# Stages of the experts in pairs, with the low parts of some first weights set apart, and two early waits

## The chip, the cores and the metric

The kernel runs on one core of a Trainium2 chip. The metric is the device time of one execution in microseconds (us). The engines are named as the profile names them: PE is TensorE (matrix products), PEld its weight loads, DVE VectorE, ACT ScalarE, POOL GpSimd, SP the engine that issues the DMAs.

## The reference

Three layers run one after the other on 1152 tokens with 512 features. The lines below are cut from the reference.

```python
# 1 attention on two batches of 8 heads: a pooled one (mean over 4) and a local one (|i-j| < 4)
out_d = sm_attn(q_d, k_d, v_d); out_up = np.repeat(out_d, factor, axis=2)
...
return (out_up + out_local).astype(np.float32)
# 2 a layer with sigmoid gating, 512 -> 2048 -> 512
h = x @ w_in
g = h * (1.0 / (1.0 + np.exp(-h)))
return (g @ w_out).astype(np.float32)
# 3 four experts, each 512 -> 1024 -> 512, weighted per token
for e in range(E):
    h = np.maximum(x @ w1[e], 0.0)
    out += p[:, e:e + 1] * (h @ w2[e])
```

## The kernel before

Every float32 operand of a product is held as two numbers of the fast type, a high part and a low part (`xh`, `xl`; `gh`, `gl`; `wh`, `wl`). One product of the mathematics is three instructions of PE: high weight by high data, high weight by low data, low weight by high data. Each instruction loads 128 columns of stationary weights and streams 256, 320 or 384 columns of moving data.

Layer 2 runs in two halves of the inner features (`for hf in range(2)`). A half goes over chunks of tokens. In a chunk, `g1_step` makes eight tiles of inner features (12 instructions each) and `g2_step` four tiles of the output (24 each). The first half has chunks of 256, 320, 256 and 320 tokens, the second of 256, 256, 256 and 384. The last tile of the first half goes into `acc` through ACT (L590), that of the second half through DVE (L593).

Layer 3 goes over experts e, chunks of tokens ci (three of 256 tokens, the last of 384) and stages k of 256 inner features. A stage has first products (`first_products`, 24 instructions on `mm` tiles, streaming `xh` and `xl`, with w1 stationary), a relu into `r` on ACT, seven linear combinations of token blocks and their high and low parts `h` on ACT, DVE and POOL, and second products (`second_products`: 21 instructions, 33 in the last chunk, with `h` stationary, streaming w2, into banks `p`). Seven block products stand for eight, so `outputs` adds the banks up on DVE with the weights of the tokens at the end of a chunk. The bank B[2] is read there last, by two adds into `u`. Only for ci = 3 do the first products stream 384 columns; these are called wide stages below. All second products stream 256.

The order on PE is: first products of stage n + 1, then second products of stage n. A scheduler moves instructions by priorities (`prio`, `tick_of`), so at the start of a chunk the two kinds are mixed in small pieces. The next expert's weights are split into high and low parts by `split_u` (w1) and `split_kk` (w2) while the wide stages run.

In the built program the stationary and moving operands have fixed places. Steps are told here by the address of the next weights less that of the moving data, modulo 128 bytes. Inside first products, inside second products and all through layer 2 the step is 64. It is 0 at each of the 105 switches from first to second products and at each of the 104 back.

Of the kernel before, what the change touches and what calls it, by code (L numbers as in the profile page):

```python
# [61 lines left out]
def attention_moe_kernel(ctx, tc, kqa, kqb, qtl, va, vb, w64, w1d, w2d, dpr, out):  # L62
# [33 lines left out]
    def prio(t):  # L96
        tc.cur_priority = 1000000 + int(1000 * t)
# [99 lines left out]
    def split_raw(u, j, t):  # L197
# [21 lines left out]
        else:  # L219
            c = slice(j * 1024, (j + 1) * 1024)  # L220
            behind(ACT, ACT.activation(out=h[:, c], in_=t, func=ACTF.Copy))
            behind(DVE, DVE.tensor_tensor(out=l[:, c], in0=t, in1=h[:, c].bitcast(F32), op=ALU.subtract))


    actx = ExitStack()
# [347 lines left out]
    def g1_step(u0, ft, o, n):  # L573
        c = slice(o, o + n)
        ps = mm_tile()
        for k in range(HP):
            mm3(ps[:, 0:n], g1_pairs(u0, ft, k, c), k == 0, k == HP - 1)
        g1_evac(ps, ft, n)

    def g2_step(u0, hf, db, o, n):  # L580
        c = slice(o, o + n)
        ps = mm_tile()
        for f in range(8):
            wh, wl = unit[u0 + f // 4]
# [14 lines left out]


    ks_p, pp_p, r_p, u_p, o_p2, h_p = [], [], [], [], [], []
    wk, w1k = {}, {}

    def tick_of(e, ci, k):
        return 96 + EXPERT * e + STAGE * (4 * ci + k) + (2 * k if ci == 3 else 0)

# [36 lines left out]
    def home_u(k):  # L643
        h, l = slot(8 + k // 2)
        c = slice(1024 * (k % 2), 1024 * (k % 2) + 1024)
        return h[:, c], l[:, c]

    def split_u(e, k):
        t, i = staged.pop((e, "u", k))
        h, l = w1k[k] = home_u(k)  # L650
        for c in (slice(0, 512), slice(512, 1024)):
            with at_prio(tick_of(e, 0, k) - LEAD_USPLIT):
                ACT.activation(out=h[:, c], in_=t[:, c], func=ACTF.Copy)
                eng = POOL if k in U_LO_POOL else DVE
                eng.tensor_tensor(out=l[:, c], in0=t[:, c], in1=h[:, c].bitcast(F32), op=ALU.subtract)
        held[i] -= 1
        stage_ahead()

# [32 lines left out]
    def first_products(st):  # L691
        e, ci, k = st.at
        t = 2 * ci
        st.r = r_p[0].tile([128, 8, 128], F32, tag="r", name="r")
        st.h = [h_p[0].tile([128, 7, 128], F32R, tag=f"h{i}", name=f"h{i}") for i in range(2)]
        if ci == 3:
            st.o = [o_p2[0].tile([128, 2, 128], F32R, tag=f"o{i}", name=f"o{i}") for i in range(2)]
            tiles = [mm_tile() for _ in range(2)]
            for half in range(2):
                prio(tick_of(*st.at) + 1.5 * half)  # L700
                m1_products(tiles[half][:, 0:384], k, half, slice(128 * t, 128 * t + 384))
        else:
            ps = mm_tile()
            for half in range(2):
                prio(tick_of(*st.at) + half)
                m1_products(ps[:, 256 * half:256 * half + 256], k, half, slice(128 * t, 128 * t + 256))
        p = tick_of(*st.at) + (3 if ci == 3 else 2) - LEAD_PAIR
        r = st.r
        with at_prio(p):
# [8 lines left out]
                                             op0=ALU.max, op1=ALU.subtract)  # L718
            else:
                ACT.activation(out=r[:, 0:4].rearrange("p s t -> p (s t)"), in_=ps[:, 0:512], func=ACTF.Relu)  # L720
        for n, (part, d) in enumerate(((slice(1, 4), 0.0), (slice(4, 8), 1.0))):
            with at_prio(p + d):
                if n == 1:
# [13 lines left out]
    def prod(ps, hs, terms, k, opens):  # L737
        wh, wl = wk[k]
        pairs = []
        for a, b in terms:  # L740
            h, l = hs[0][:, a], hs[1][:, a]
            pairs += [(h, wh[:, b]), (h, wl[:, b]), (l, wh[:, b])]
        n = len(pairs)
        ins = [PE.matmul(out=ps, lhsT=x, rhs=y, start=(opens and k == 0 and i == 0), stop=(k == 3 and i == n - 1),  # L744
                         skip_group_check=True) for i, (x, y) in enumerate(pairs)]
        return ins[0]

    def second_products(st, ch):
        e, ci, k = st.at
# [9 lines left out]
        first = {}  # L759
        for t, i, hs, terms in groups:  # L760
            m = prod(half(t, i), hs, terms, k, i == 0)
            if k == 0:
                if i == 0:
                    first[id(t)] = m
                else:
                    after(m, first[id(t)])

    def scaled_add(o, ps, p, first=False):
        if first:
# [155 lines left out]
    class Chunk:  # L925
        pass

    def finish(st, ch, p):
        e, ci, k = st.at
        prio(p)  # L930
        second_products(st, ch)
        if ci == 3 and e < NE - 1:
            split_kk(e + 1, k)
            if k < 2:
                sum_ahead(e + 1, k + 2)
        if k == 3:
            outputs(e, ci, ch, p)

    before = None
    for e in range(NE):  # L940
        for ci in range(4):
            ch = Chunk()
            for k in range(4):
                st = Stage()
                st.at = (e, ci, k)
                first_products(st)
                if ci == 3 and e < NE - 1:
                    split_u(e + 1, k)
                if ci == 2 and k % 2 == 0 and e < NE - 1:
                    sum_ahead(e + 1, k // 2)  # L950
                if before:
                    finish(*before, tick_of(e, ci, k) + (3 if ci == 3 else 2))
                before = (st, ch)
    finish(*before, tick_of(NE, 0, 0) + 2)


# [54 lines left out]
```

## Time and profile before

| What | Value |
|---|---|
| median of 3 runs | 679.53 us (675.22 to 679.6) |
| the profiled execution | 679.06 us, its span 677.1 us |
| granted TensorE clock, mean | 0.989 |
| PE busy | 652.2 us, 96% of the span |
| layer 2, second half | about 188 to 290 us of the span |
| the experts | about 290 to 670 us |

The span runs from the first to the last instruction; the rest of the execution's time lies outside it. PE has an instruction in flight nearly all the time, so its busy share does not tell how fast it goes. What tells it is the distance from one start of a PE instruction to the next, which is read from the start times of the timeline.

### The profile page before, as it was taken

The numbers are of one execution on the slowest core, as the hardware profiler recorded it, in microseconds if no ns is written. First come the engines' busy times: TensorE is split into PE (matmuls) and PEld (weight loads), VectorE is DVE, ScalarE is ACT, GpSimd is POOL, SyncE is SP. The second block draws the span as 40 slices with busy tenths as digits, with TensorE's granted clock in tenths as the row PEclk, the third lists the DMA queues.
The fourth block names the chain that finished last, engine by engine and source line by source line (L and its number), as shares of the span: only waits on it lengthen the run. The fifth ranks groups of instructions, "written<-read, shape, count | busy, mean of one in ns | idle before, by whom it ended". The sixth has DMA issues, their size and how long they took to land.

```text
span 677.1 us, 13739 instructions
## 1 busy us (share of the span) xinstructions
PE 652.2 (96%) x5516; PEld 636.4 (94%) x5516; DVE 418.6 (62%) x850; ACT 330.6 (49%) x753; POOL 245.1 (36%) x346
## 2 busy tenths in 40 slices
PE   4879999999999999999999999999999999999995
PEld 4668988998999999999999999999999999999995
DVE  4668575474645544765548865668854668755434
ACT  2898765478844434352335633346533356433321
POOL 5536641133600000652356323545422554333210
PEclk9898999999999999999999999999999999999998
DMA  8964612116501200140003310013300020000001
GB/s 265 364 224 146 210 39 62 25 47 203 170 18 32 94 1 1 63 156 1 1 1 100 119 33 1 1 32 125 95 1 1 1 64 1 1 33 32 1 32 47
DMA packets 16927, 48.16 MB, mean 71 GB/s; under 512 B 2976, under 2 KB 4256, under 8 KB 16864
## 3 DMA queue, kind: packets, MB, share of 16 engines
q1 hardware_dynamic: 16864, 47.29, 21.8%
q8 instruction: 43, 0.70, 0.4%
q14 instruction: 20, 0.16, 0.1%
HBM read 44.93 MB, written 2.36 MB: 70 GB/s over the span
## 4 chain that ended last, share of the span: by engine, by line
PE 82%; DMA 5%; ACT 4%; DVE 4%; POOL 3%; issue 1%; SPq 0%; ACTq 0%; POOLq 0%
PE mm L540 53%; PE p L744 26%; DMA stg<-in_w_dram 3%; DVE dec L210 1%; DMA vg_f<-in_va_dram 1%; ACT dec L208 1%; PE s L369 1%; DMA vg<-in_va_dram 1%; POOL wbuf L218 1%; POOL kq L306 1%; PE t L432 1%; DVE acc L772 1%; PE o L464 1%; ACT wbuf L217 0%; ACT stg L209 0%
## 5 line engine op out<-in xcount | busy, mean ns | idle before, releaser
L540 PE MATMUL mm<-xh,wbuf 128*128 128x256 f32 (+2 forms) x1280 | 269.4, 297 | 5.5 <-DVE gf L560 3.6
L540 PEld LDWEIGHTS mm<-xh,wbuf 128*128 128x128 f32 x1280 | 210.9, 190 | 7.7 <-DVE gf L560 5.2
L540 PE MATMUL mm<-xl,wbuf 128*128 128x256 f32 (+2 forms) x640 | 189.6, 297 | 0.0
L726 POOL TENSOR_TENSOR r<-r 128x128 f32<-128x128 f32 x160 | 93.4, 596 | 183.7 <-ACT r L720 144.1
L729 DVE TENSOR_TENSOR h<-r,h 128x384 fp32r<-128x384 f32 (+1 forms) x128 | 91.7, 720 | 64.6 <-ACT h L728 64.3
L540 PEld LDWEIGHTS mm<-xl,wbuf 128*128 128x128 f32 x640 | 121.6, 190 | 0.2
L728 ACT ACTIVATE h<-r 128x384 fp32r<-128x384 f32 (+1 forms) x128 | 73.2, 577 | 85.0 <-POOL r L726 53.9
L540 PE MATMUL mm<-gh,wbuf 128*128 128x256 f32 (+2 forms) x512 | 103.5, 296 | 1.0 <-DVE gf L560 0.9
L744 PE MATMUL p<-wext,h 128*128 128x256 f32 x672 | 91.5, 279 | 0.0
L744 PE MATMUL p<-wbuf,h 128*128 128x256 f32 x672 | 84.6, 278 | 0.0
L744 PEld LDWEIGHTS p<-wext,h 128*128 128x128 f32 x672 | 84.4, 188 | 0.0
L540 PEld LDWEIGHTS mm<-gh,wbuf 128*128 128x128 f32 x512 | 82.3, 188 | 1.5 <-DVE gf L560 1.1
L744 PEld LDWEIGHTS p<-wbuf,h 128*128 128x128 f32 x672 | 81.2, 188 | 0.0
L540 PE MATMUL mm<-gl,wbuf 128*128 128x256 f32 (+2 forms) x256 | 74.2, 295 | 0.0
L720 ACT ACTIVATE r<-mm 128x512 f32<-128x512 f32 x48 | 28.7, 597 | 76.1 <-PE mm L540 75.7
L726 DVE TENSOR_TENSOR r<-r 128x128 f32<-128x128 f32 x96 | 33.6, 351 | 37.6 <-ACT r L720 33.0
L566 DVE TENSOR_TENSOR gl<-gf,gh 128x256 fp32r<-128x256 f32 (+2 forms) x64 | 37.6, 589 | 18.9 <-ACT gh L565 18.1
L540 PEld LDWEIGHTS mm<-gl,wbuf 128*128 128x128 f32 x256 | 47.8, 188 | 0.0
L218 POOL TENSOR_TENSOR wbuf<-dec,wbuf 128x512 fp32r<-128x512 f32 x24 | 32.0, 1351 | 24.9 <-ACT wbuf L217 18.8
L772 DVE SCALAR_TENSOR_TENSOR acc<-p,pr,acc 128x256 f32<-128x256 f32 (+1 forms) x63 | 36.1, 605 | 5.9 <-PE p L744 5.9
L671 POOL TENSOR_TENSOR wext<-kst,wext 128x512 fp32r<-128x512 f32 x8 | 10.7, 1342 | 79.9 <-ACT wext L669 44.3
L560 DVE SCALAR_TENSOR_TENSOR gf<-th,mm 128x256 f32<-128x256 f32 (+2 forms) x64 | 28.4, 450 | 17.7 <-ACT th L559 16.2
(138 smaller groups left out, 940.8 us busy)
## 6 DMA issues: line engine op xcount, KB each, us to landing
stg<-in_w_dram SPq DMA_DIRECT2D x25, 512.0 KB
kst<-in_w2d_dram SPq DMA_DIRECT2D x16, 512.0 KB
kst<-in_w1d_dram SPq DMA_DIRECT2D x12, 512.0 KB
acc<-in_w_dram SPq DMA_DIRECT2D x7, 512.0 KB
kq<-in_kqb_dram SPq DMA_DIRECT2D x8, 323.0 KB
kq<-in_kqa_dram SPq DMA_DIRECT2D x6, 419.0 KB
stg<-in_w1d_dram SPq DMA_DIRECT2D x4, 512.0 KB
vw<-in_vb_dram SPq DMA_DIRECT2D x8, 180.0 KB
```

The source lines that it names most:

```text
L208: first = ACT.activation(out=d, in_=v[:, :, 1].bitcast(F32), func=ACTF.Prelu, scale=2.0 ** -112, alpha=2.0 ** 32)
L218: POOL.tensor_tensor(out=l[:, c], in0=d, in1=h[:, c].bitcast(F32), op=ALU.subtract)
L540: ins = [PE.matmul(out=ps, lhsT=l, rhs=r, start=(first and i == 0), stop=(last and i == n - 1)) for i, (l, r) in enumerate(pairs)]
L560: DVE.scalar_tensor_tensor(out=gf[:, 0:n], in0=th[:, 0:n], scalar=1.0, in1=ps[:, 0:n], op0=ALU.add, op1=ALU.mult)
L566: latest[DVE] = DVE.tensor_tensor(out=gl[ft][:, 0:n], in0=gf[:, 0:n], in1=gh[ft][:, 0:n].bitcast(F32), op=ALU.subtract)
L671: b = eng.tensor_tensor(out=l[:, r], in0=x, in1=h[:, r].bitcast(F32), op=ALU.subtract)
L720: ACT.activation(out=r[:, 0:4].rearrange("p s t -> p (s t)"), in_=ps[:, 0:512], func=ACTF.Relu)
L726: latest[eng] = eng.tensor_tensor(out=r[:, o], in0=r[:, a], in1=r[:, b], op=op)
L728: ACT.activation(out=h, in_=r[:, part], func=ACTF.Copy)
L729: latest[DVE] = DVE.tensor_tensor(out=l, in0=r[:, part], in1=h.bitcast(F32), op=ALU.subtract)
L744: ins = [PE.matmul(out=ps, lhsT=x, rhs=y, start=(opens and k == 0 and i == 0), stop=(k == 3 and i == n - 1), skip_group_check=True) for i, ...
L772: DVE.scalar_tensor_tensor(out=o, in0=ps, scalar=p, in1=o, op0=ALU.mult, op1=ALU.add)
```

## The change

Four things change. Stages go in pairs: first products of two stages, then second products of the pair before, in a fixed order (`emit` chains every product of layer 3 behind the one before). That leaves 31 switches from first to second products and 30 back. For the first stage of each pair, the low part of its first 128 columns of w1 is written into a place of its own (`first_lo`), and that product goes first, so that the step at all 30 switches back is 64. The relu, the combinations and the `o` buffers (three now) follow the pairs. And the last tile of each half of layer 2 is moved out of PSUM in two parts, of 16 columns and the rest; the first product of the second half, and the first of the experts, waits for the 16 columns.

```diff
-            mm3(ps[:, 0:n], g1_pairs(u0, ft, k, c), k == 0, k == HP - 1)
+            i, _ = mm3(ps[:, 0:n], g1_pairs(u0, ft, k, c), k == 0, k == HP - 1)
+            if k == 0 and part_done:
+                wait_part(i)
         g1_evac(ps, ft, n)
...
+    part_done = []
+
+    def wait_part(i):
+        tc.add_manual_dep(i.ins, part_done.pop().ins.name, mybir.DependencyInfo(mybir.DependencyClass.Sync, mybir.DependencyReason.DATA),
+                          reason="part done")
...
+        last = db == 3 and o + n == NT
+        cols = (slice(0, 16), slice(16, n)) if last else (slice(0, n),)
         if hf == 0:
-            ACT.activation(out=ya, in_=ps[:, 0:n], func=ACTF.Copy, scale=0.5)
+            done = [ACT.activation(out=ya[:, a], in_=ps[:, a], func=ACTF.Copy, scale=0.5) for a in cols]
         else:
             yf = tmp_p[0].tile([128, tmp_p[1]], F32, tag="gf", name="gf")
-            DVE.scalar_tensor_tensor(out=yf[:, 0:n], in0=ps[:, 0:n], scalar=0.5, in1=ya, op0=ALU.mult, op1=ALU.add)
+            done = [DVE.scalar_tensor_tensor(out=yf[:, a], in0=ps[:, a], scalar=0.5, in1=ya[:, a], op0=ALU.mult, op1=ALU.add)
+                    for a in cols]
+        if last:
+            part_done[:] = done[:1]
...
+    def apart(k):
+        return k % 2 == 0
+
+    PAIRS = [((e, ci, k), (e, ci, k + 1)) for e in range(NE) for ci in range(4) for k in (0, 2)]
+
+    def product_ticks():
+        at, t = {}, 96
+        for n in range(len(PAIRS) + 1):
+            for what, pair in (("m", n), ("p", n - 1)):
+                for x in PAIRS[pair] if 0 <= pair < len(PAIRS) else ():
+                    at[what, x] = t
+                    t += 3 if x[1] == 3 else 2
+        return at
+
+    AT = product_ticks()
...
+    def lower(eng, k, l, h, t, c):
+        parts = [(l[:, c], c)]
+        if apart(k) and c.start == 0:
+            parts = [(w1a[k], slice(0, 128)), (l[:, 128:c.stop], slice(128, c.stop))]
+        return [eng.tensor_tensor(out=o, in0=t[:, s], in1=h[:, s].bitcast(F32), op=ALU.subtract) for o, s in parts]
...
-    def m1_products(ps, k, half, c):
+    def m1_products(ps, k, half, c, begin=False):
         wh, wl = w1k[k]
+        pairs = []
         for q in range(HP):
             s = slice(half * 512 + q * 128, half * 512 + q * 128 + 128)
-            mm3(ps, [(wh[:, s], xh[:, q, c]), (wh[:, s], xl[:, q, c]), (wl[:, s], xh[:, q, c])], q == 0, q == HP - 1)
+            if apart(k) and half == q == 0 and not begin:
+                pairs += [(w1a[k], xh[:, q, c]), (wh[:, s], xh[:, q, c]), (wh[:, s], xl[:, q, c])]
+            else:
+                pairs += [(wh[:, s], xh[:, q, c]), (wh[:, s], xl[:, q, c]), (wl[:, s], xh[:, q, c])]
+        n = len(pairs)
+        return [lambda i=i, a=a, b=b: PE.matmul(out=ps, lhsT=a, rhs=b, start=(i == 0), stop=(i == n - 1))
+                for i, (a, b) in enumerate(pairs)]
...
+        first_lo = late.tile([128, 384], F32R, name="first_lo")
+        for i in range(2):
+            w1a[2 * i] = first_lo[:, 80 + 128 * i:208 + 128 * i]
...
-    o_p2.append(moe2_pool("o2", 2))
+    o_p2.append(moe2_pool("o2", 3))
...
+    newest = []
+
+    def emit(todo, t):
+        with at_prio(t):
+            for f in todo:
+                i = f()
+                if newest:
+                    follow(i, newest[0], "order of products")
+                else:
+                    wait_part(i)
+                newest[:] = [i]
...
+    def second_stage(at):
+        e, ci, k = at
+        st = stages[at]
+        t = AT["p", at]
+        emit(second_products(st, st.ch), t)
+        prio(t)
...
+    for n in range(len(PAIRS) + 1):
+        new = []
+        if n < len(PAIRS):
+            new.append(first_stage(PAIRS[n][0]))
+            first_relu(new[0])
+            new.append(first_stage(PAIRS[n][1]))
+        for i in range(2):
+            if n:
+                second_stage(PAIRS[n - 1][i])
+            if new:
+                if i == 0:
+                    first_relu(new[1])
+                first_results(new[i])
```

On PE, at a switch from second to first products in the first expert, the rows before are these (`p` are the banks, `mm` the tile of the first products).

```order
L744 MATMUL p_4126<-wbuf,h_4208 128x256 x2
L744 MATMUL p_4126<-wbuf,h_4209 128x256
L540 MATMUL mm<-xh,wbuf 128x256
L540 MATMUL mm<-xl,wbuf 128x256
L540 MATMUL mm<-xh,wbuf 128x256 x2
```

The switch falls after second products of one stage, on weights in `wbuf`. After, at the first such switch, PE's rows are these.

```order
L797 MATMUL p_3937<-wext,h_3873 128x256 x2
L797 MATMUL p_3937<-wext,h_3874 128x256
L727 MATMUL mm<-xh,first_lo 128x256
L727 MATMUL mm<-xh,wbuf 128x256
L727 MATMUL mm<-xl,wbuf 128x256
```

The first product after the switch now takes its weights from `first_lo`, and the two with the high part follow; before it, second products of two stages stand in a row.

On DVE, at the end of the first expert's last chunk, from the first add into `u` that reads bank p_4656 (B[2]) to the second, the rows before are these (`acc<-` are the scaled adds, `wbuf<-` weight splits for the next expert, `h` a low part).

```order
L801 TENSOR_TENSOR u<-u,p_4656 128x256
L729 TENSOR_TENSOR h_4902<-r,h_4901 128x512
L671 TENSOR_TENSOR wbuf<-ks,wbuf 128x256
L772 SCALAR_TENSOR_TENSOR acc<-p_4657,pr,acc 128x256
L772 SCALAR_TENSOR_TENSOR acc<-p_4655,pr,acc 128x256
L772 SCALAR_TENSOR_TENSOR acc<-p_4657,pr,acc 128x512
L671 TENSOR_TENSOR wbuf<-ks,wbuf 128x512
L671 TENSOR_TENSOR wbuf<-kst,wbuf 128x512
L772 SCALAR_TENSOR_TENSOR acc<-u,pr,acc 128x256
L729 TENSOR_TENSOR h_4994<-r,h_4993 128x384
L805 TENSOR_TENSOR u<-u,p_4656 128x256
```

Nine operations stand between the two, no combination `r<-r` among them. After, the last part of the same stretch on DVE, with p_4736 as B[2], is this.

```order
L782 TENSOR_TENSOR h_5027<-r,h_5026 128x384
L833 SCALAR_TENSOR_TENSOR acc<-p_4737,pr,acc 128x256
L833 SCALAR_TENSOR_TENSOR acc<-p_4735,pr,acc 128x256
L833 SCALAR_TENSOR_TENSOR acc<-p_4737,pr,acc 128x512
L782 TENSOR_TENSOR h_5027<-r,h_5026 128x512
L709 TENSOR_TENSOR wbuf<-kst,wbuf 128x512
L779 TENSOR_TENSOR r<-r 128x128
L833 SCALAR_TENSOR_TENSOR acc<-u,pr,acc 128x256
L779 TENSOR_TENSOR r<-r 128x128 x2
L866 TENSOR_TENSOR u<-u,p_4736 128x256
```

Three combinations `r<-r` now stand ahead of the second add into `u`, where there were none.

On ACT, at the end of the first half of layer 2, the rows before are these.

```order
L590 ACTIVATE acc<-mm 128x320
L217 ACTIVATE wbuf<-dec 128x512
L590 ACTIVATE acc<-mm 128x320 x3
L559 ACTIVATE th<-mm 128x256
L565 ACTIVATE gh_2625<-gf 128x256
```

The four tiles of the last chunk leave in four operations. After, ACT's rows at that place are these.

```order
L602 ACTIVATE acc<-mm 128x320
L217 ACTIVATE wbuf<-dec 128x512
L602 ACTIVATE acc<-mm 128x320 x2
L602 ACTIVATE acc<-mm 128x16
L602 ACTIVATE acc<-mm 128x304
L561 ACTIVATE th<-mm 128x256
```

The last of the four tiles is moved in two parts.

## Rows read from the trace of the kernel before

**Rows 1.** The page: busy time by engine, and the chain that ended last.
```profile
PE 652.2 (96%) x5516; PEld 636.4 (94%) x5516; DVE 418.6 (62%) x850; ACT 330.6 (49%) x753; POOL 245.1 (36%) x346
...
PE 82%; DMA 5%; ACT 4%; DVE 4%; POOL 3%; issue 1%; SPq 0%; ACTq 0%; POOLq 0%
```

**Rows 2.** PE's timeline, first expert: start us, us, then line, names, shape, count.
```profile
321.45 2.64 PE L744 MATMUL p<-wext,h 128*128 128x256 f32 x21
...
323.92 0.28 PE L540 MATMUL mm<-xh,wbuf 128*128 128x256 f32 x1
...
326.65 2.55 PE L744 MATMUL p<-wbuf,h 128*128 128x256 f32 x21
...
329.04 0.28 PE L540 MATMUL mm<-xh,wbuf 128*128 128x256 f32 x1
...
331.87 2.64 PE L744 MATMUL p<-wbuf,h 128*128 128x256 f32 x21
```

**Rows 3.** PE's timeline where the second half starts and its last chunk starts.
```profile
188.04 0.31 PE L540 MATMUL mm<-gh,wbuf 128*128 128x320 f32 x1
...
188.18 0.28 PE L540 MATMUL mm<-xh,wext 128*128 128x256 f32 x1
...
256.03 0.34 PE L540 MATMUL mm<-xh,wext 128*128 128x384 f32 x1
```

**Rows 4.** PE's timeline after a wide stage, in the first and last expert.
```profile
354.25 2.63 PE L744 MATMUL p<-wbuf,h 128*128 128x256 f32 x21
...
356.71 0.34 PE L540 MATMUL mm<-xh,wbuf 128*128 128x384 f32 x1
...
662.25 1.22 PE L744 MATMUL p<-wbuf,o 128*128 128x256 f32 x9
...
666.14 1.22 PE L744 MATMUL p<-wbuf,o 128*128 128x256 f32 x9
```

**Rows 5.** Busy time in a stretch: PE, PEld, DVE, ACT, POOL, clock, DMA, GB/s.
```profile
300.00:350.00 50.00, 50.00 (x432) 50.00 (x432) 29.27 (x55) 18.42 (x34) 19.32 (x32) 1.00 0.01 2
```

**Rows 6.** PE's timeline after a wait, and after a break of other matmuls.
```profile
65.99 0.39 PE L540 MATMUL mm<-gh,wbuf 128*128 128x256 f32 x1 [0.86 <-DVE gf L560]
...
132.18 0.40 PE L540 MATMUL mm<-gh,wbuf 128*128 128x320 f32 x1
...
133.34 0.39 PE L540 MATMUL mm<-xh,wbuf 128*128 128x256 f32 x2
...
133.68 0.39 PE L540 MATMUL mm<-xh,wbuf 128*128 128x256 f32 x2
```

**Rows 7.** The timeline of all engines, where a tile leaves PSUM and PE waits.
```profile
188.38 0.44 ACT L590 ACTIVATE acc<-mm 128x320 f32<-128x320 f32 x1 [3.08 <-PE mm L540]
...
289.77 0.56 DVE L593 SCALAR_TENSOR_TENSOR gf<-mm,acc 128x384 f32<-128x384 f32 x1 [1.87 <-PE mm L540]
...
162.82 0.47 DVE L560 SCALAR_TENSOR_TENSOR gf<-th,mm 128x320 f32<-128x320 f32 x1
...
163.35 0.19 PEld L540 LDWEIGHTS mm<-xh,wbuf 128*128 128x128 f32 x1 [0.28 <-DVE gf L560]
```

**Rows 8.** Groups by line and form: busy us, mean ns; idle before.
```profile
L712 ACT ACTIVATE r<-mm 128x256 f32<-128x256 f32 x32 | 11.9, 372 | 15.8 <-PE mm L540 14.3 <-DVE acc L772 1.5
...
L716 ACT ACTIVATE o<-mm 128x128 fp32r<-128x128 f32 x32 | 8.7, 271 | 0.0
...
L717 DVE SCALAR_TENSOR_TENSOR o<-mm,o 128x128 fp32r<-128x128 f32 x32 | 9.1, 285 | 21.7 <-ACT o L716 21.7
...
L726 DVE TENSOR_TENSOR r<-r 128x128 f32<-128x128 f32 x96 | 33.6, 351 | 37.6 <-ACT r L720 33.0 <-ACT r L712 3.3
```

**Rows 9.** The timeline of DVE and PE, end of the first expert.
```profile
386.65 1.41 DVE L770 TENSOR_SCALAR acc<-p,pr 128x512 f32<-128x512 f32 x2 [0.33 <-PE p L744]
...
387.47 0.28 PE L540 MATMUL mm<-xh,wbuf 128*128 128x256 f32 x1
...
393.64 0.41 DVE L805 TENSOR_TENSOR u<-u,p 128x256 f32<-128x256 f32 x1
```

More of the change, by code (lines that the diff above doesn't have):

```diff
@@ L221, in split_raw @@
             behind(ACT, ACT.activation(out=h[:, c], in_=t, func=ACTF.Copy))
-            behind(DVE, DVE.tensor_tensor(out=l[:, c], in0=t, in1=h[:, c].bitcast(F32), op=ALU.subtract))
+            k = 2 * (u - 8) + j
+            for o, a in ((l[:, c], slice(0, 1024)),) + (((w1a[k], slice(0, 128)),) if apart(k) else ()):
+                behind(DVE, DVE.tensor_tensor(out=o, in0=t[:, a], in1=h[:, c][:, a].bitcast(F32), op=ALU.subtract))
     actx = ExitStack()
@@ L601, in attention_moe_kernel @@
     ks_p, pp_p, r_p, u_p, o_p2, h_p = [], [], [], [], [], []
-    wk, w1k = {}, {}
+    wk, w1k, w1a = {}, {}, {}
+    def apart(k):
[10 more added lines that the diff above has]
+    AT = product_ticks()
     def tick_of(e, ci, k):
-        return 96 + EXPERT * e + STAGE * (4 * ci + k) + (2 * k if ci == 3 else 0)
+        return 96 + EXPERT * NE if e == NE else AT["m", (e, ci, k)]
     todo = deque([(0, "k", k) for k in range(4)])
@@ L654, in split_u @@
                 eng = POOL if k in U_LO_POOL else DVE
-                eng.tensor_tensor(out=l[:, c], in0=t[:, c], in1=h[:, c].bitcast(F32), op=ALU.subtract)
+                lower(eng, k, l, h, t, c)
         held[i] -= 1
@@ L693, in first_products, with first_relu @@
         t = 2 * ci
+        if ci == 3:
+            st.tiles = [mm_tile() for _ in range(2)]
+            return [i for half in range(2)
+                    for i in m1_products(st.tiles[half][:, 0:384], k, half, slice(128 * t, 128 * t + 384))]
+        st.tiles = [mm_tile()]
+        return [i for half in range(2)
+                for i in m1_products(st.tiles[0][:, 256 * half:256 * half + 256], k, half, slice(128 * t, 128 * t + 256), (e, ci) == (0, 0))]
+    def first_relu(st):
+        e, ci, k = st.at
+        tiles = st.tiles
+        ps = tiles[0]
         st.r = r_p[0].tile([128, 8, 128], F32, tag="r", name="r")
-        st.h = [h_p[0].tile([128, 7, 128], F32R, tag=f"h{i}", name=f"h{i}") for i in range(2)]
         if ci == 3:
             st.o = [o_p2[0].tile([128, 2, 128], F32R, tag=f"o{i}", name=f"o{i}") for i in range(2)]
[L698 to L706, printed above, removed]
         p = tick_of(*st.at) + (3 if ci == 3 else 2) - LEAD_PAIR
@@ L720, in first_products, with first_results @@
                 ACT.activation(out=r[:, 0:4].rearrange("p s t -> p (s t)"), in_=ps[:, 0:512], func=ACTF.Relu)
+    def first_results(st):
+        e, ci, k = st.at
+        r = st.r
+        st.h = [h_p[0].tile([128, 7, 128], F32R, tag=f"h{i}", name=f"h{i}") for i in range(2)]
+        p = tick_of(*st.at) + (3 if ci == 3 else 2) - LEAD_PAIR
         for n, (part, d) in enumerate(((slice(1, 4), 0.0), (slice(4, 8), 1.0))):
@@ L743, in prod @@
         n = len(pairs)
-        ins = [PE.matmul(out=ps, lhsT=x, rhs=y, start=(opens and k == 0 and i == 0), stop=(k == 3 and i == n - 1),
-                         skip_group_check=True) for i, (x, y) in enumerate(pairs)]
-        return ins[0]
+        return [lambda i=i, x=x, y=y: PE.matmul(out=ps, lhsT=x, rhs=y, start=(opens and k == 0 and i == 0),
+                                                stop=(k == 3 and i == n - 1), skip_group_check=True)
+                for i, (x, y) in enumerate(pairs)]
     def second_products(st, ch):
@@ L758, in second_products, with opening @@
             groups.insert(5, (B[3], 1, st.o, ((0, 2),)))
-        first = {}
+        first, todo = {}, []
+        def opening(f, t, i):
+            m = f()
+            if i == 0:
+                first[id(t)] = m
+            else:
+                after(m, first[id(t)])
+            return m
         for t, i, hs, terms in groups:
-            m = prod(half(t, i), hs, terms, k, i == 0)
+            fs = prod(half(t, i), hs, terms, k, i == 0)
             if k == 0:
[L763 to L766, printed above, removed]
+                fs[0] = lambda f=fs[0], t=t, i=i: opening(f, t, i)
+            todo += fs
+        return todo
     def scaled_add(o, ps, p, first=False):
@@ L926, in attention_moe_kernel, with first_stage @@
         pass
[L928 to L931, printed above, removed]
+    newest = []
[5 more added lines that the diff above has]
+                    follow(i, newest[0], "order of products")
+                else:
+                    wait_part(i)
+                newest[:] = [i]
+    stages = {}
+    def first_stage(at):
+        e, ci, k = at
+        st = stages[at] = Stage()
+        st.at = at
+        st.ch = stages[e, ci, 0].ch if k else Chunk()
+        emit(first_products(st), tick_of(*at))
+        if ci == 3 and e < NE - 1:
+            split_u(e + 1, k)
+        if ci == 2 and k % 2 == 0 and e < NE - 1:
+            sum_ahead(e + 1, k // 2)
+        return st
+    def second_stage(at):
+        e, ci, k = at
+        st = stages[at]
+        t = AT["p", at]
+        emit(second_products(st, st.ch), t)
+        prio(t)
         if ci == 3 and e < NE - 1:
@@ L936, in finish @@
         if k == 3:
[L937 to L954, printed above, removed]
+            outputs(e, ci, st.ch, t)
+    for n in range(len(PAIRS) + 1):
[8 more added lines that the diff above has]
+            if new:
+                if i == 0:
+                    first_relu(new[1])
+                first_results(new[i])
 def kernel(**inputs):
```

1 line of the change is left out of this document (added).

## The prediction

> **What bounds the kernel now.** The page comes first: PE is busy 96% of the span, and 82% of the chain that ended last is PE [rows 1]. So the time is PE's, and the question is how far apart its products start. In the timeline of PE in the first expert, 21 second products from 321.45 us to 323.92 take 117.6 ns each, the 24 first products after them 113.8, the next 21 second products 113.8 and the 24 first products from 329.04 to 331.87 117.9 [rows 2]. Shapes and engine are the same, and the clock stays at 1.00, the upper level of 2.4 GHz [rows 5]. So there are two paces. A settled fast row of products has three products in 0.34 us, 113.3 ns each [rows 6]; the slow pace is read best from the second half of layer 2, where 576 products of 256 columns go from 188.18 to 256.03, 117.8 ns each, all slow [rows 3].
>
> What sets the pace? It lasts through steps of 64 and through the switches from first to second products: the stretch at 326.65 stays fast, as the one before it [rows 2]. It turns at switches back, slow to fast at 323.92 and fast to slow at 329.04 [rows 2]; of 46 such switches with a clear pace on both sides, all 15 out of the fast pace end slow, 20 of 31 out of the slow one end fast. After a wide stage it is slow in all 16 cases: 21 products at 117.1 ns after the first one, 33 at 117.9 after the last [rows 4]. From 320 columns straight into 256 it is slow too [rows 3], but after the same 320 columns and a break of other matmuls it is fast at 133.34 [rows 6]. In the experts the two paces mix: 432 products overlap 50 us, (50 + 0.28) / 432 = 116.4 ns [rows 5].
>
> **The change, part by part,** in the span of the profiled execution (677.1 us, with 1.96 us outside it).
>
> *The wait at the second half.* PE now stops before 188.18. The last product starts at 188.04 and takes 0.31 us [rows 3], ACT starts at 188.38 on the tile [rows 7]; 16 columns take about 0.18 us by the line through 128 columns (271 ns) and 256 (372 ns) [rows 8]. A released PE loads weights 0.06 us after the releaser's end (162.82 + 0.47 to 163.35, [rows 7]), and its product starts some 0.11 us later. That gives 188.73, 0.55 us late; the first starts after a stop are about 0.12 us slower in sum than settled ones. Price 0.67 us. ACT was idle for 3.08 us before [rows 7], so nothing stands ahead of it; on PE the whole second half is queued behind the wait. Bounds: 0.6 us, and 0.8 if 16 columns cost as much as 128. In return the half starts after a stop, so fast if the break at 132 us is the pattern: 576 x (117.8 - 113.3) = 2.6 us less. Its 384-column chunk I leave as it is.
>
> *The wait at the experts.* The same on DVE, which starts at 289.77 after 1.87 us of idling and takes 0.56 us for 384 columns [rows 7], 285 ns for 128 [rows 8], so about 0.17 for 16. Price 0.66 us. The two waits make +1.3 us.
>
> *The switches.* All 30 switches back now have the step of 64 that never turned the pace, and the 31 others never did. So a pace stays until a wide stage or a stop. With 256 columns an expert has 3 x 4 x 24 = 288 first and 12 x 21 + 4 x 33 = 384 second products, 672 in all, 2688 in four. The first expert starts fast and keeps it for 288 first products and ten stages of 21 second ones, 498 products; the first wide stage makes it slow.
>
> *A stop at the ends of experts.* Seen in the order on DVE: the sixth group of the next expert's first second products opens bank B[2], which DVE must have read twice. In the trace that queue, 13 operations, runs from 386.65 to 393.64 + 0.41, 7.4 us; first products went on at 387.47 [rows 9]. After, the same 13 and three combinations of 351 ns [rows 8] stand there, some 0.3 us each as neighbours overlap: 8.3 us, and two operations that stood behind the first scaled add now precede the second, so that it starts at about the end of PE's products, not 0.8 us before. PE arrives after 48 first and 15 second products, 63 x 117.8 ns = 7.4 us. So it waits 8.3 + 0.2 (restart as above) - 7.4 = 1.1 us, between 0 (the old lead of 0.8 us and quicker splits) and 1.6 (PE fast, 0.3 us earlier). Three such ends: +3.3 us, 0 to 4.8. At the other chunk ends the queue lacks the three splits and a scaled add, four of sixteen, so about 6.2 us against 7.4, and no stop.
>
> Each such stop also restarts PE fast. A later expert then is slow from its predecessor's wide stages to the stop (42 + 66 + 48 + 66 + 48 + 15 = 285) and fast for the other 387. With the last expert's 42 + 132 at the end: 498 + 3 x 387 = 1659 fast and 1029 slow. 1659 x 113.3 + 1029 x 117.8 = 309.2 us, against 2688 x 116.4 = 312.9: -3.7 us.
>
> *Nothing on the path:* the low parts in two pieces (some 8 more operations of 0.2 to 0.6 us on DVE and POOL, which are busy 62% and 36% [rows 1]); the pairs, which give the results of a stage more time before PE needs them. Without that cover each piece would cost its length.
>
> Sum: -2.6 + 1.3 + 3.3 - 3.7 = -1.7; 679.06 - 1.7 = **677.4 us**. The profiled execution is 0.5 us under the median of 679.53. With the bounds of the stops, 674 to 680.
>
> **A rule against the change.** The rows show two paces for the same shapes [rows 2]. The Trainium skill, page SBUF — State Buffer, section "A bandwidth-pool intuition that's wrong (but worth ruling out)", gives weight loads a second read port of their own. By that rule the place of weights cannot disturb the moving data, and setting some apart buys no pace. No row here shows ports; by it the sum would be that of the fourth rival.
>
> **The rivals.** *Fast nearly throughout.* Wide stages left it slow, but each was entered slow; entered fast, or with `first_lo` after it, the pace may hold. Then 2688 x 3.1 ns = 8.3 us less: -2.6 + 1.3 - 8.3 = -9.6 without stops (669.5 us), -5.4 with three of 1.4 (673.7). Against it: 16 of 16 [rows 4].
>
> *Slow to the end.* The stops are hidden, or a restart amid second products is not fast: from the first wide stage 2190 products are slow, +3.1 - 1.5 = +1.6: 679.4 without stops, 682.7 with them.
>
> *Slower: the new step holds the slow pace.* Fast or slow may hang on more than the step modulo 128: inside second products it is 192 or 448 modulo 512, inside first ones 64, and no row shows the one follow the other directly. If `first_lo` ends the fast pace at the first switch back, 96 first and 42 second products are fast and some 2550 slow, +3.6 - 0.4, and with a second half that stays slow too: +1.3 + 3.2 + 3.3 = 686.9 us. This decides once more than about 1900 of the 2688 products are slow.
>
> *Places don't matter.* The mix of 116.4 ns stays, and the second half is slow by chance: +1.3 + 3.3 = 683.7 us. The runs before, from 675.22 to 679.6, allow for such chance.
>
> **How the numbers follow.** Chances: forecast 0.43, fast nearly throughout 0.2, slow to the end 0.2, the new step 0.1, places 0.07. Predicted 677.4; the range runs from 671 (most of the fast case) to 685.5 (all but the new step). A measurement of this kernel tells about 1% from no change, so faster means under 672.7, slower over 686.3: 0.15 (half the fast case and a tail), 0.08 (the new step and a tail), and 0.77 between.
>
> **What would show it.** In the profile after: a gap of some 0.55 us before the first product on `wext` and products 113.3 ns apart behind it, up to the 384-column chunk; a like gap at the experts, and 42 second products at 113.3 behind 96 first ones; slow second products after the first wide stage; a wait of PE for DVE's add into `u` about 1 us long at three ends of experts, and fast products behind it. The prediction is wrong if wide stages leave PE fast, if no such wait is there, or if first products behind `first_lo` change pace.

## The result and the profile after

The changed kernel takes 688.21 us (median of 4 runs, 687.0 to 688.71), the kernel before 679.57 us. The ratio is 1.014, with a 95% interval from 1.0097 to 1.0183. Beside later kernels it was timed once more, at 685.6 us against 678.25, ratio 1.0094 (1.0062 to 1.0126). So it is slower by about 1%. The forecast of 677.4 us was wrong; what came is the third rival, the new step that holds the slow pace (686.9 us).

The profiled execution took 688.2 us, its span 686.4. First the page, busy time by engine and the chain that ended last, as in [rows 1]:

```profile
PE 656.9 (96%) x5516; PEld 638.6 (93%) x5516; DVE 419.0 (61%) x856; ACT 327.8 (48%) x754; POOL 243.8 (36%) x349
...
PE 79%; DVE 7%; DMA 6%; ACT 3%; POOL 2%; issue 1%; SPq 0%; ACTq 0%; POOLq 0%; DVEq 0%
```

PE's share is the same 96%, for a span that is 9.3 us longer. As before, the share doesn't tell the pace. PE's timeline tells it. These rows are the two new waits and the first switches of the experts (start us, us, line, names, shape, count; idle time before and its releaser):

```profile
190.73 0.30 PE L542 MATMUL mm<-gh,wbuf 128*128 128x320 f32 x1
191.31 0.38 PE L542 MATMUL mm<-xh,wext 128*128 128x256 f32 x1 [0.27 <-ACT acc L602]
...
291.09 0.34 PE L542 MATMUL mm<-gh,wbuf 128*128 128x384 f32 x1
291.69 0.39 PE L727 MATMUL mm<-xh,wbuf 128*128 128x256 f32 x1 [0.27 <-DVE gf L605]
...
302.70 4.92 PE L797 MATMUL p<-wext,h 128*128 128x256 f32 x42
307.46 0.28 PE L727 MATMUL mm<-xh,first_lo 128*128 128x256 f32 x1
...
313.11 5.11 PE L797 MATMUL p<-wbuf,h 128*128 128x256 f32 x42
318.06 0.28 PE L727 MATMUL mm<-xh,first_lo 128*128 128x256 f32 x1
...
323.71 5.11 PE L797 MATMUL p<-wext,h 128*128 128x256 f32 x42
```

Two things are read here. A row of 42 second products is 4.92 us long in the fast pace and 5.11 in the slow one. And the starts give the pace of first products: 96 from 291.69 to 302.70 (114.7 ns with the restart), 42 second ones from 302.70 to 307.46 (113.3), then the first product on `first_lo`, and from there 48 in 5.65 us (117.7 ns), 42 in 4.95 (117.9), 48 in 5.65. The fast pace ends exactly at the first switch back. It comes back once in the rest of the experts, for 90 products, besides some seven just before the first stop.

The waits of PE that the change brought, in the view of waits (waited for: us in total, times, longest), and PE at the end of the first expert:

```profile
PE p L797 <- DVE u L866: 3.6, 3, 1.2
...
PE mm L542 <- ACT acc L602: 0.6, 2, 0.3
...
PE mm L727 <- DVE gf L605: 0.3, 1, 0.3
```

```profile
398.51 1.90 PE L797 MATMUL p<-wext,h 128*128 128x256 f32 x15
401.65 3.45 PE L797 MATMUL p<-wext,h 128*128 128x256 f32 x27 [1.24 <-DVE u L866]
```

The stop at the end of an expert is there, after the 15 products that the prediction named. From product 15 to product 16 pass 1517 ns, and 227 to the next. On DVE, the queue behind which PE waited starts and ends with these rows, and the first of them stands ahead of it:

```profile
392.52 1.78 DVE L709 TENSOR_TENSOR wbuf<-kst,wbuf 128x512 fp32r<-128x512 f32 x1
394.22 1.40 DVE L831 TENSOR_SCALAR acc<-p,pr 128x512 f32<-128x512 f32 x2
...
401.19 0.41 DVE L866 TENSOR_TENSOR u<-u,p 128x256 f32<-128x256 f32 x1
```

Where the 9.3 us lie, worked out from starts. (a) Up to the last product before the second half the two kernels run the same instructions in the same order, and yet it starts at 190.73 instead of 188.04 [rows 3]: 2.7 us. The windows over the first 66 us, ahead of layer 2 (PE busy, count, clock, DMA share, GB/s), are those of the kernel before, of the changed one, and of the changed one in its second profiled execution (run 9):

```profile
0.00:66.00 66.00, 49.91 (x483) 0.92 0.75 251
```

```profile
0.00:66.00 66.00, 49.64 (x463) 0.87 0.72 239
```

```profile
0.00:66.00 66.00, 52.28 (x497) 0.87 0.75 252
```

The granted clock is lower in the changed kernel, 0.87 against 0.92, that is, more of the time at 1.2 GHz. But it is 0.87 in run 9 too, and there the same kernel reached the second half at 188.79. So the mean clock doesn't explain the 2.7 us, and what does isn't shown. They are chance, not the change: one kernel differs by 2.5 us from itself, and over all profiles here the second half starts at 186.4 to 193.5 us. (b) The two waits: 0.58 us instead of 0.14 before the second half, 0.60 instead of 0.17 before the experts, and 0.1 more for the product behind each: 1.1 us. (c) The second half, without what (b) counts of it: 99.9 us against 101.4, 1.5 less. It starts in the slow pace (191.31), although after a stop, and turns fast right behind two breaks of 0.1 us each, at 219.6 and 219.8. (d) The three stops: 4.5 us. (e) The pace of the experts: the 256-column products stand 117.4 ns apart in the mean, 116.4 before: 2688 x 0.95 = 2.5 us more. Sum: 2.7 + 1.1 - 1.5 + 4.5 + 2.5 = 9.3. Without (a) 6.6 us are left, near the 7.35 us between the medians of the second timing.

### The profile page after: what moved, and what is told of

It reads as the page before. It is cut to its first block, busy times and chain, and to the rows that moved or that the text cites. A ratio compares the mean times of both kernels' runs of the same rounds, so it can differ in the third digit from the quotient of the medians.

```text
span 686.4 us, 13849 instructions
## 1 busy us (share of the span) xinstructions
PE 656.9 (96%) x5516; PEld 638.6 (93%) x5516; DVE 419.0 (61%) x856; ACT 327.8 (48%) x754; POOL 243.8 (36%) x349
## 4 chain that ended last, share of the span: by engine, by line
PE 79%; DVE 7%; DMA 6%; ACT 3%; POOL 2%; issue 1%; SPq 0%; ACTq 0%; POOLq 0%; DVEq 0%
PE mm L727 27%; PE p L797 24%; PE mm L542 24%; DMA stg<-in_w_dram 3%; DVE acc L833 2%; DMA qt<-in_qtl_dram 2%; DVE wbuf L709 1%; PE s L371 1%; DVE h L782 1%; PE t L434 1%; DMA kq_f<-in_kqa_dram 1%; ACT dec L208 1%; DVE dec L210 1%; PE o L466 1%; POOL wbuf L218 1%
## 5 line engine op out<-in xcount | busy, mean ns | idle before, releaser
L727 PE MATMUL mm<-xh,wbuf 128*128 128x256 f32 (+1 forms) x994 | 201.9, 295 | 0.3 <-DVE gf L605 0.3
L727 PEld LDWEIGHTS mm<-xh,wbuf 128*128 128x128 f32 x994 | 162.1, 189 | 0.6 <-DVE gf L605 0.6
L779 POOL TENSOR_TENSOR r<-r 128x128 f32<-128x128 f32 x160 | 89.7, 574 | 177.6 <-ACT r L767 127.5
L727 PE MATMUL mm<-xl,wbuf 128*128 128x256 f32 (+1 forms) x512 | 149.9, 295 | 0.0
L782 DVE TENSOR_TENSOR h<-r,h 128x384 fp32r<-128x384 f32 (+1 forms) x128 | 88.1, 704 | 89.7 <-ACT h L781 89.7
L781 ACT ACTIVATE h<-r 128x384 fp32r<-128x384 f32 (+1 forms) x128 | 67.1, 570 | 78.6 <-PE p L797 75.3
L727 PEld LDWEIGHTS mm<-xl,wbuf 128*128 128x128 f32 x512 | 96.1, 188 | 0.0
L797 PE MATMUL p<-wext,h 128*128 128x256 f32 x672 | 84.3, 280 | 3.6 <-DVE u L866 3.6
L797 PEld LDWEIGHTS p<-wext,h 128*128 128x128 f32 x672 | 81.2, 188 | 4.3 <-DVE u L866 4.3
L542 PE MATMUL mm<-xh,wbuf 128*128 128x256 f32 (+1 forms) x256 | 56.6, 306 | 4.2 <-DVE gf L562 2.8
L568 DVE TENSOR_TENSOR gl<-gf,gh 128x256 fp32r<-128x256 f32 (+2 forms) x64 | 39.3, 617 | 19.3 <-ACT gh L567 18.6
L542 PEld LDWEIGHTS mm<-xh,wbuf 128*128 128x128 f32 x256 | 43.0, 194 | 6.4 <-DVE gf L562 4.4
```

What stands on the lines that cost most here:

```text
L542: ins = [PE.matmul(out=ps, lhsT=l, rhs=r, start=(first and i == 0), stop=(last and i == n - 1)) for i, (l, r) in enumerate(pairs)]
L568: latest[DVE] = DVE.tensor_tensor(out=gl[ft][:, 0:n], in0=gf[:, 0:n], in1=gh[ft][:, 0:n].bitcast(F32), op=ALU.subtract)
L727: return [lambda i=i, a=a, b=b: PE.matmul(out=ps, lhsT=a, rhs=b, start=(i == 0), stop=(i == n - 1)) for i, (a, b) in enumerate(pairs)]
L779: latest[eng] = eng.tensor_tensor(out=r[:, o], in0=r[:, a], in1=r[:, b], op=op)
L781: ACT.activation(out=h, in_=r[:, part], func=ACTF.Copy)
L782: latest[DVE] = DVE.tensor_tensor(out=l, in0=r[:, part], in1=h.bitcast(F32), op=ALU.subtract)
```

## The experiments

Times are medians; the ratio is to the kernel before, timed beside them (678.97 us for the first four, 679.36 for the next four, 678.25 for the last four). "Pace" is the mean distance of the 256-column products of the experts, stops left out.

**1. Without `first_lo`.**

```diff
     def apart(k):
-        return k % 2 == 0
+        return False
```

> The changed kernel without first_lo (every first stage of a pair uses the usual order and place of its low part; pairs, fixed order and both waits stay), so the step at the 30 switches back is 0 again. Theory H (the product on first_lo holds the slow pace and ends the fast one): switches back turn the pace again, all out of fast and two thirds out of slow, which leaves about 40% of some 2550 products of the experts fast, 0.4 x 2550 x 4.5 ns = 4.6 us less than the changed kernel, about 683.6 us, and the trace shows fast stretches in every expert. Rival R (first_lo has no part in it; wide stages, stops and the long fixed stretches keep the pace slow): 688.2 us, experts at 117.8 ns as before.

685.12 us, ratio 1.0081 (1.0048 to 1.0113). The rows of PE, first expert:

```profile
303.20 4.92 PE L797 MATMUL p<-wext,h 128*128 128x256 f32 x42
307.96 0.28 PE L727 MATMUL mm<-xh,wbuf 128*128 128x256 f32 x1
...
318.56 0.28 PE L727 MATMUL mm<-xh,wbuf 128*128 128x256 f32 x1
```

The switch at 307.96 still ends the fast pace, but the one at 318.56 turns it back (42 second products from 324.02 are fast again). Of the switches back between clear stretches of 256 columns, 10 of 10 out of fast end slow and 11 of 12 out of slow end fast. In the changed kernel it was 2 of 2 and only 1 of 20. The pace is 116.0 ns instead of 117.4. So H's mechanism is shown, but for one thing: the switch back ends the fast pace with `first_lo` or without it, and what `first_lo` took away is the turn from slow to fast. The edit also puts the product with the low part back behind the two others, so its place and its turn in the order aren't told apart here (run 8 moves the place alone). H's 683.6 us isn't quite reached, because PE now arrives faster at the ends of experts and stops there for longer (5.5 us in all instead of 4.5). By the medians alone the two kernels (1.0081, and 1.0094 to 1.014) can't be told apart for certain; the rows can.

**2 to 4. Second products 64 bytes further on.** In the built program w2 moves 64 bytes further on; h and o move 64 bytes back, which is the same modulo 128. So all steps of the experts are 64 modulo 128: in the kernel before, in it with the two waits, and in the changed kernel without `first_lo`. (`u5` moves too, by 128 bytes, as the tile before it grew.)

```diff
-        b, o = (wext[0], 2 * KF * k) if k < 2 else (wbuf, 2 * UW * (k - 2))
+        b, o = (wext[0], 2 * KF * k + 16) if k < 2 else (wbuf, 2 * UW * (k - 2) + 16)
...
+    moe2_pool("gap_h", 1).tile([128, 16], F32, name="gap_h")
```

> The kernel before with the weights w2 of the second products and their stationary tiles h and o each 64 bytes further on: both kinds of products then stream from places that are 0 modulo 128 and load weights that are 64, and all 209 switches have a step of 64. Theory A (the pace turns where the moving data starts 64 bytes off the stretch before, modulo 128): no switch turns it any more; the experts inherit the slow pace of the second half and keep it, 2688 x (117.8 - 116.4) ns = 3.8 us more, 683.4 us. Rival B (the step alone decides, 0 or 64, whatever streams): the same, as all steps are 64, but then the changed kernel's slow switches stay unexplained. Rival C (places don't matter): the mix of 116.4 ns stays, 679.6 us.

> The same shift, with the two waits of the change added (the last tile of each half of layer 2 in parts of 16 columns and the rest, the first product of the second half and of the experts behind the first part). The waits cost 1.2 us. Theory A: the pace at the start of the experts, fast after the wait as in the changed kernel, is kept through every switch: 679.6 + 1.2 - 2688 x 3.1 ns = 672.5 us if wide stages keep it too, and about 682.4 us if the first wide stage makes it slow and nothing turns it back; the second half is slow or partly fast, up to 2.6 us less. Rival C: mix, 680.8 us.

> The changed kernel without first_lo and with the shift of w2, h and o by 64 bytes: pairs, fixed order, both waits, and every switch with a step of 64 and no change of the start of the moving data modulo 128. Theory A: the experts start fast and the 61 switches keep it: 688.2 - 2550 x 4.5 ns = 676.7 us if wide stages keep the pace, about 686.6 us if they make it slow for good (only some 360 more fast products than in the changed kernel). Rival R or C: 688.2 us, the experts at 117.8 ns.

679.77 us (1.0014, 0.9978 to 1.005), 680.52 us (1.0006, 0.9978 to 1.0033) and 685.19 us (1.0072, 1.0041 to 1.0104). Theory A fell. The first two times are those of rival C (679.6 and 680.8 us), but the rows speak against it too. PE in the third of them:

```profile
297.02 5.11 PE L797 MATMUL p<-wext,h 128*128 128x256 f32 x42
301.97 0.28 PE L727 MATMUL mm<-xh,wbuf 128*128 128x256 f32 x1
...
307.43 5.11 PE L797 MATMUL p<-wbuf,h 128*128 128x256 f32 x42
312.38 0.28 PE L727 MATMUL mm<-xh,wbuf 128*128 128x256 f32 x1
```

The experts started fast here, and the first switch from first to second products, which out of the fast pace had always kept it, now made it slow: 9 of 9 such switches out of fast, while all 11 out of slow (without those into a stretch with a stop) became fast. The switch back turns it as well: 48 first products from 301.97 take 5.46 us (113.7 ns). So places do matter, against rival C, but the step modulo 128 isn't what counts. In this kernel the steps at the switches are 192 modulo 256, inside either kind 64.

**5 to 7. All places alike modulo 256.** The same edit with 48 columns (192 bytes) for 16, and 512 bytes more for `wext`, so that what lies behind it (`u5` and the buffers of the splits) keeps its place modulo 256. w2 moves 192 bytes on, h and o 192 back. Moving data then starts at 128 and weights at 192 modulo 256 in both kinds, so the step is 64 modulo 256 everywhere, at the switches too. (Steps of 64 inside both kinds and at the switches are only to be had with both kinds at the same places.)

> The kernel before with w2, h and o 192 bytes further on instead of 64: moving data of all products is then at 128 and weights at 192 modulo 256, in both kinds alike (in the kernel before second products have them the other way round, at 192 and 128; with 64 bytes they had 0 and 64), and every step is 64 modulo 256. Theory A2 (the pace turns at a switch where the two kinds differ modulo 256, whatever the step modulo 128): no switch turns it; the experts take over the slow pace of the second half and keep it: 679.0 + 2688 x (117.8 - 116.4) ns = 682.8 us, nearly no fast stretch in the experts. Rival B2 (a switch of kind turns it as such, by the other bank or the other tile that is written): toggling goes on, the mix of 116.4 ns, 679 to 680 us.

> The same places, with the two waits of the change. Theory A2: the pace that follows the wait at the experts is kept to the end. If it is fast and wide stages keep it: 679.0 + 1.2 - 2688 x 3.1 ns = 671.9 us, down to 669.3 with a fast second half; if the wait leaves it slow: some 684 us. Rival B2: the mix, about 680 us.

> The changed kernel without first_lo, with w2, h and o 192 bytes further on (pairs, fixed order and both waits stay). Theory A2: fast after the wait at the experts, kept through 61 switches and the wide stages: 688.2 - 2550 x 4.5 ns = 676.7 us; what then stays over the kernel before is the three stops and the waits. If the pace after a stop is slow, it stays slow to the end: up to 685. Rival B2: as the changed kernel without first_lo, 685 us, with fast and slow stretches in turn.

670.1 us, ratio 0.9892 (0.982 to 0.9963); with the waits 671.49, 0.9893 (0.986 to 0.9925); in the changed kernel 678.92, 0.9979 (0.9943 to 1.0015). PE around two wide stages, in the first of them:

```profile
343.34 2.54 PE L744 MATMUL p<-wbuf,h 128*128 128x256 f32 x21
345.72 0.33 PE L540 MATMUL mm<-xh,wbuf 128*128 128x384 f32 x1
...
349.88 2.55 PE L744 MATMUL p<-wbuf,h 128*128 128x256 f32 x21
352.26 0.33 PE L540 MATMUL mm<-xh,wbuf 128*128 128x384 f32 x1
```

21 products in 2.38 us, 24 wide ones in 4.16 (173.3 ns), 21 in 2.38: fast before, inside and after. Before, the 24 wide ones that start at 356.71 [rows 4] last to 360.91, 175.0 ns each, and the slow pace follows them. In the three profiles every switch keeps the fast pace, and the pace of the experts is 113.4 ns, all through. Rival B2 fell. The stops keep it too; PE at the first one in the changed kernel with places alike:

```profile
391.33 2.44 PE L797 MATMUL p<-wext,h 128*128 128x256 f32 x15
394.99 3.35 PE L797 MATMUL p<-wext,h 128*128 128x256 f32 x27 [1.22 <-DVE u L866]
```

The 27 products behind the stop are 3.35 us long, 3.45 in the changed kernel. The windows over 30 us (PE busy, count, clock, DMA share, GB/s), of the kernel before, of the changed one and of the first of these three:

```profile
410.00:440.00 30.00, 30.00 (x261) 1.00 0.00 1
```

```profile
310.00:340.00 30.00, 30.00 (x257) 1.00 0.01 1
```

```profile
410.00:440.00 30.00, 30.00 (x267) 1.00 0.00 1
```

A2's rule held, its first forecast did not: without the waits the experts were to inherit the slow pace (682.8 us), but the second half had turned fast before its end, at 215.5 us, where its weights change from `wext` to `u`, with no break longer than 10 ns. The other two forecasts, 671.9 and 676.7 us, came within 2.3 us. Each profile is one execution, in runs 5 and 7 the fastest (667.2 of 667.2 to 675.91 us, 674.03 of 674.03 to 686.05); whether a slower one entered the experts in the slow pace, and kept it, isn't shown. The last two differ in the pairs alone (with the order of products and the `o` buffers that belong to them), at the same pace and with the same waits. From the experts' start to PE's last product pass 371.5 us without pairs and 377.7 with them. The stops and restarts of the latter sum to 6.2 us (the medians are 7.4 apart). So the pairs cost their stops, in full, and brought nothing else.

**8. `first_lo` in another place.**

```diff
-            w1a[2 * i] = first_lo[:, 80 + 128 * i:208 + 128 * i]
+            w1a[2 * i] = first_lo[:, 112 + 128 * i:240 + 128 * i]
```

> The changed kernel with first_lo 128 bytes further on, nothing else: the step at the 30 switches back is 192 modulo 256, as inside the second products, instead of 64. Theory A2: a product at any odd place doesn't make the two kinds alike, so the pace still turns or is lost at switches: 683 to 688 us. Rival D (the place of first_lo was only chosen badly; the step must be that of the products just before): the fast pace after the wait lasts to the wide stages, and to the end if these keep it: 676.7 to 686.5 us, with fast first products behind first_lo at the first switch back.

684.89 us, ratio 1.0091 (1.0057 to 1.0126). PE at the first switch back:

```profile
299.58 4.92 PE L797 MATMUL p<-wext,h 128*128 128x256 f32 x42
304.34 0.28 PE L727 MATMUL mm<-xh,first_lo 128*128 128x256 f32 x1
```

48 first products from 304.34 take 5.65 us: slow again. All 7 switches back out of fast end slow, 6 of 15 out of slow become fast (1 of 20 in the changed kernel, 3 of 18 in run 9). Rival D fell: one product at another place doesn't carry the fast pace over.

**9 and 10. The changed kernel again, and without its stops.**

```diff
-LO_ON_POOL = ((0, 0), (1, 0), (2, 0), (3, 0))
+LO_ON_POOL = ((0, 0), (1, 0), (2, 0), (3, 0), (3, 1), (3, 2), (3, 3))
```

> The changed kernel itself, beside the next three on the same chip, so that they can be set against it. Both theories: 1.01 to 1.018 of the kernel before, about 688 us.

> The changed kernel with three more low parts of the last w2 piece made by POOL instead of DVE (0.33, 0.6 and 0.6 us on DVE, which stood ahead of the last read of B[2] at the ends of experts); places, pairs and waits are as in the changed kernel. If the three stops of 1.4 us and their restarts are paid in full: no wait for the add into u at the ends of experts, 688 - 4.6 = 683.6 us. Rival (the stops only move, POOL's slower operation or another bank is late next): a wait of about the same length on another releaser, 687 to 689 us. The pace stays slow in either case.

685.6 us (1.0094) and 685.23 us (1.0094, 1.0061 to 1.0127). The first is under the 688 us that both theories gave. In the views of waits, the changed kernel and then the one without its stops:

```profile
PE p L797 <- DVE u L866: 3.7, 3, 1.2
```

```profile
PE p L797 <- ACT h L781: 0.6, 1, 0.6
```

The stops at the ends of experts are gone, but the medians don't show it, so the 683.6 us of the one theory weren't met. From the experts' start to PE's last product it is 384.8 us instead of 387.0, 2.1 less and not 4.6. A new stop of 1.4 us with its restarts stands in the first chunk at 305.3 us, where ACT waits for a combination of POOL, which now has the low parts to make. And the pace is slower, 117.45 instead of 117.1 ns (0.9 us), because in run 9 the switch behind each of the three stops had turned it fast for a while. Both theories are right in part. Why the 2.1 us don't appear in the medians stays open; the chance of (a) is larger than that.

**11. The kernel before with the two waits alone.**

> The kernel before with the two waits alone (16-column parts and the first products behind them; no pairs, no first_lo, places as before). The waits cost 2 x 0.6 us; the second half, 576 products of 256 columns, is faster by up to 2.6 us if it starts fast, by nothing if it starts slow again: 677.9 to 680.5 us at 679.3 before. In the experts the mix of paces stays (116.4 ns). Rival (the waits themselves bring the slow experts): 682 to 685 us.

680.44 us, ratio 1.0014 (0.999 to 1.0039), pace 116.3 ns. The waits aren't what makes the experts slow, and alone they neither gain nor lose what can be measured.

**12. All places alike and only the wait at the second half.**

> The kernel before with all places alike modulo 256 (w2, h and o 192 bytes further on) and only the wait at the second half. Theory A2: the fast pace lasts from the wait or from a later break in the second half to the end: 679.3 - 8.3 (experts) - 0.9 (wide stages, 192 and 96 products of 384 columns at 173.3 instead of 174.7 to 176.7) - up to 2.6 + 0.6 = 668 to 671 us, the same as with both waits or up to 0.6 us less. If the wait leaves the second half slow and nothing turns it: 680 us or more.

670.94 us, ratio 0.9874 (0.9805 to 0.9943), as with both waits or with none. PE at the start of the second half, of its 384-column chunk and of the experts, then a row of the experts:

```profile
188.70 0.38 PE L540 MATMUL mm<-xh,wext 128*128 128x256 f32 x1 [0.27 <-ACT acc L600]
...
256.65 0.34 PE L540 MATMUL mm<-xh,wext 128*128 128x384 f32 x1
...
289.93 0.28 PE L540 MATMUL mm<-xh,wbuf 128*128 128x256 f32 x1
...
306.37 2.54 PE L758 MATMUL p<-wbuf,h 128*128 128x256 f32 x21
```

576 products from 188.70 to 256.65 are 118.0 ns apart: the wait left the pace slow, and places alike don't mend it by themselves. The 384-column chunk then ran fast (192 in 33.28 us, 173.3 ns), and the experts after it to the end: a row of 21 second products is 2.54 us long, 2.64 in the slow pace [rows 2]. So these three kernels (runs 5, 6 and 12), 1.1 to 1.3% faster than the kernel before and 2 to 2.6% faster than the changed one, are the ones to keep; between them the runs don't decide.

## Why the prediction was wrong

*The step that failed* is that of the switches: "All 30 switches back now have the step of 64 that never turned the pace ... So a pace stays until a wide stage or a stop." The step was counted modulo 128. Modulo 256 it is 64 inside first products and 192 inside second ones, and a switch stands between the two whatever the step at it. The fast pace lasted 96 + 42 products instead of 498. In every profile with these places the switch back ended it, whatever its step: 0 (run 1, 10 of 10), 64 (2 of 2 and, in run 9, 4 of 4) and 192 (run 8, 7 of 7). In the kernel before the turn was more regular than the prediction's "20 of 31" says: counted between stretches of at least ten products of 256 columns, all 14 switches back out of fast end slow and all 17 out of slow end fast. `first_lo` took nearly all of the latter away. The rest of the forecast for the experts (1659 fast products, -3.7 us) hung on it; measured is +2.5 us, 6.2 us beside the sum. The third rival named this very gap ("it is 192 or 448 modulo 512, inside first ones 64, and no row shows the one follow the other directly") and had a chance of 0.1. Its "some 2550 slow" is met nearly word for word. Its price was a little high, +3.2 us against +2.5, as one stop did turn the pace for 90 products. That its 686.9 us is nearly the measured time is partly luck: the start (a) is over it by 2.7 us, the second half under it by 1.5.

*Each stop also restarts PE fast:* wrong. All three left it slow, the first one although the products just before it were fast; behind one of them the next switch turned it. With these places it is so in all profiles, 13 of 13 stops (the changed kernel, runs 1, 8, 9 and 10), while the three stops of run 7 and two of the three of run 4 leave it fast. The second rival had named it, "a restart amid second products is not fast".

*The wait at the second half, and its gain:* the waits cost 1.1 us against 1.3. The gain of 2.6 us was 1.5 here, and came behind the breaks inside the half, not from the wait. Of the eleven profiles with this wait PE comes out of it fast in seven (runs 3, 4, 6, 7, 8, 9 and 11) and slow in four (the changed kernel, runs 1, 10 and 12). Runs 6, 7 and 11 gave back the 2.6 us; run 9 (101.2 us, with the wait at its end) turned slow at the same breaks and gave back about 0.7.

*The stops:* right in place, number and releaser; in size +4.5 us against +3.3, inside the bounds of 0 to 4.8. Each is 1.5 us with its restart, against 1.1. Two terms of the working were off, in opposite ways. The 16 operations on DVE take 7.4 us, from 394.22 to 401.60, as the 13 did before, and not 8.3. But they start 1.4 us after PE's first products went on (392.86) and not with them, because the split of 1.78 us from 392.52 stands ahead.

*After wide stages slow, 16 of 16:* a true count, and no property of wide stages. Run 5 leaves all 16 of them fast.

*The rule against the change.* That places alone, with the order of instructions kept, take the pace of the experts from 116.4 ns to 113.4 (run 5) isn't what the prediction drew from the Trainium skill, page SBUF — State Buffer, section "A bandwidth-pool intuition that's wrong (but worth ruling out)", with its second read port for weight loads. The measurement decides: places do set the pace. Run 5 moves what second products stream (w2) and their weights (h, o) together, so whether weight loads disturb the moving data isn't shown.

*What stays open.* Why a difference modulo 256 acts as it does isn't shown: with the places of the kernel before, the switch from first to second products keeps the pace and the one back turns it, while 64 bytes further on both turn it. Whether the equal places or the step of 64 everywhere keeps the pace isn't shown either, since the one brings the other. And a step of 64 throughout doesn't fix the pace: in the second half of layer 2, where all steps are 64 modulo 256 in the kernel before and in runs 5 and 12, it is slow to the end of the 256-column products in two of them and turns fast at 215.5 us in run 5.

## What to carry to other kernels

When PE is busy all the time, measure the distance of its starts by stretches before moving work: two paces of one shape 4% apart hide behind 96%. When a rule for places is read from a trace, look at them modulo a larger number too, and prefer to make all of them alike over mending the one place where they meet; here that was two offsets and two pads. An order that gathers the work of two stages also gathers what reads their results, so look for the last reader of each bank that the next group opens.

## What was not expected of the hardware

PE has two paces for 256 columns, 113.3 and 117.8 ns at a clock of 1.00, and whether it keeps the fast one depends on where weights and moving data lie modulo 256 bytes: with both kinds at the same places and a step of 64 throughout, every switch and wide stage of four profiles, which all entered the experts fast, kept 113.3 ns to the end. Two breaks of 0.1 us can turn the pace (at 219.6 and 219.8 us in the changed kernel), and the wait at the second half, 0.44 us longer than before, left it slow in four of eleven profiles. And two executions of the changed kernel reached the second half 2.5 us apart, at 191.31 and 188.79.
